# Loading the first tiles of x and w1 in another order and on other queues

## The chip, the core and the metric

The kernel runs on one core of one Trainium2 chip. The metric is the device time of one execution in microseconds (us). The engines that matter here are TensorE (PE, with weight loads on a lane of their own, PEld), VectorE (DVE), ScalarE (ACT) and the sync engine (SP), which issues transfers. Every load is done by 16 DMA engines; SP and ScalarE each have an issuing queue (q1 and q10 in the profile).

## What is computed

A gate mixes a linear-attention block with a token-mixing MLP over the same x (2048 tokens, 512 features, bf16):

```
g = sigmoid((x * gate_w).sum(-1, keepdims=True))
a = linear_attention(x, wqkv) @ wo         # 32 heads of 16, phi = elu + 1
h = layernorm(x)                           # over the 512 features
u = gelu(einsum("bsd,sf->bdf", h, w1) + b1)    # w1 is 2048 x 1792
y = einsum("bdf,fs->bds", u, w2) + b2
return g * a + (1 - g) * transpose(y)
```

The part around the change is the layer norm and the first product, h with w1, summed over the 2048 tokens.

## The kernel before

The 2048 tokens are cut into 16 tiles of 128 (`NT`). `xr` holds x, `xh` the normalised x, both 128 x 512 per tile. The columns of w1 are cut in two: `w1A` holds the first 1024 (`FA`), `w1B` the other 768, which come much later. A tile of x is 128 KB, a tile of `w1A` 256 KB. A product needs one tile of x and the same tile of w1.

**Loads.** All are recorded by the helper `load` (line 124), on SP unless another engine is named. An issue on SP takes about 0.43 us. ScalarE's queue holds, in order: a one-element square root (line 135) that brings in the activation table; the rows of b1 (136); the first 128 columns of w1's tiles 0 and 1 (137, 138). SP's queue holds x0, x1, the other 896 columns of w1's tile 0 (142), and then the loop of lines 143 to 151: x2, the rest of w1's tile 1, x3, w1's tile 2, x4, w1's tile 3, and so on, with the rows of b2 behind w1's tile 4. So every x tile from 2 on is one w1 tile ahead of its own partner. Then come the gate's row, wk, a transposed x, `w1B` and other weights.

**Order.** The order on each engine is written by hand: `tc.keep_in_program_order` (`pin`) holds every instruction where it stands. SP issues in order too, and an issue can wait for an older transfer to land.

**Layer norm.** DVE takes the tiles in turn (lines 195 to 236). `ln_bn` makes the statistics (line 198), `ln_aggr` gathers them (201) and ScalarE takes the square root (203), `ln_apply` makes the reciprocal (209) and writes `xh` (211). For tiles 1 to 3 the statistics come in two halves, and the work on the tile before is put between them. The order on DVE is therefore

```
bn(1, first half), apply(0), bn(1, second half), aggr(1),
bn(2, first half), apply(1), bn(2, second half), aggr(2),
bn(3, first half), apply(2), ...
```

At tile 8 four transposes (line 233) turn the bias rows into columns.

**Matmuls.** TensorE first runs 18 matmuls on a constant (line 189) that nothing reads. Then, for tiles 0 to 11, eight matmuls per tile (lines 276 to 278) add up into eight PSUM banks `accA`, one for each 128 columns of `w1A`; tiles 12 to 15 follow bank by bank (279 to 282), each bank ending in a gelu. All matmuls are recorded on line 74. After that come k and its products with x (`kacc`, `Gps`), the other w1 columns (`accB`), q (`qacc`), and the last stage with w2 (`yps`).

Of the kernel before, what the change touches and what calls it, by code (L numbers as in the profile page):

```python
# [7 lines left out]
ACT = mybir.ActivationFunctionType  # L8
ALU = mybir.AluOpType
AX = mybir.AxisListType  # L10
BF16 = mybir.dt.bfloat16
# [4 lines left out]
def kernel(  # L16
# [13 lines left out]
    nc = tc.nc  # L30
    P = nc.NUM_PARTITIONS
# [9 lines left out]
    NT = S // P  # L41
    ND = D // P
    NF = F // P
# [4 lines left out]
    FA = NFA * P  # L48
# [5 lines left out]
    w1_view = B_w1.rearrange("(t p) f -> p t f", p=P)  # L54
    w2_view = B_w2.rearrange("(f p) s -> p f s", p=P)
    b1_view = B_b1.rearrange("(f p) -> f p", p=P)
# [9 lines left out]
    def ptile(shape, dt, name):  # L66
        return persist.tile(shape, dt, name=name, tag=name)
# [27 lines left out]
    b_rows = ptile([32, P], BF16, "b_rows")  # L95
# [15 lines left out]
    eps_t = ptile([P, 1], FP32, "eps_t")  # L111
# [6 lines left out]
    w1A = wpool.tile([P, NT, FA], BF16, name="w1A", tag="w1st")  # L118
    w1B = wpool.tile([P, NT, F - FA], BF16, name="w1B", tag="w2nd")

    pin = tc.keep_in_program_order

    def load(o, i, eng=None, **kw):
        pin((eng or nc.sync).dma_start(out=o, in_=i, **kw))

    def load_x(t0, t1):
        load(xr[:, t0:t1, :], x_view[:, t0:t1, :])

    def load_w1a(t):
        load(w1A[:, t, :], w1_view[:, t, 0:FA])  # L130


    tbl = work.tile([P, 1], FP32, name="tbl", tag="tbl", bufs=2)
    unit = nc.const_aps.tensor(1.0, [P, 1], BF16)
    pin(nc.scalar.activation(out=tbl[:], in_=unit, func=ACT.Sqrt))
    load(b_rows[0:NF, :], b1_view, nc.scalar)
    load(w1A[:, 0, 0:P], w1_view[:, 0, 0:P], nc.scalar)
    load(w1A[:, 1, 0:P], w1_view[:, 1, 0:P], nc.scalar)

    load_x(0, 1)  # L140
    load_x(1, 2)
    load(w1A[:, 0, P:FA], w1_view[:, 0, P:FA])
    for t in range(1, NT):
        if t + 1 < NT:
            load_x(t + 1, t + 2)
        if t == 1:
            load(w1A[:, 1, P:FA], w1_view[:, 1, P:FA])
        else:
            load_w1a(t)
        if t == 4:  # L150
            load(b_rows[NF : NF + NT, :], b2_view)
    load(gw_b[:], gw_row_view.to_broadcast([P, D]))
    load(wk_sb[:], wqkv_view[:, :, D : 2 * D])
# [12 lines left out]
    for j in range(ND):  # L166
# [9 lines left out]
        out=mask[:], in_=mask[:], compare_op=ALU.is_gt, fill=1.0,  # L176
# [3 lines left out]
        out=mask[:], in_=mask[:], compare_op=ALU.is_ge, fill=0.0,  # L180
# [58 lines left out]
    tbl = work.tile([P, 1], FP32, name="tbl", tag="tbl", bufs=2)  # L239
# [98 lines left out]
    for i in range(ND):  # L338
# [4 lines left out]
            out=z_parts[:, 1, :], in0=zacc[:], in1=z_parts[:, 0, :], op=ALU.subtract  # L343
# [222 lines left out]
    t = NT - 1  # L566
# [35 lines left out]
```

## Time and profile before

| what | us |
|---|---|
| median of 3 runs | 162.99 (162.88 to 163.32) |
| the profiled execution | 163.58 |
| its span, first to last instruction | 161.8 |
| TensorE busy | 158.0 |
| VectorE busy | 118.7 |
| ScalarE busy | 53.1 |
| first matmul of `accA` | 4.91 |
| last matmul of `accA` ends | 33.51 |

Times in the views are from the start of the span. The span is 1.8 us shorter than the execution's own time, since it leaves out what lies before the first and after the last instruction. The timeline lists instructions by start and length; in brackets stands idle time ahead of one and what ended it. The chain of waits goes back from the last instruction to whatever released it. The table of stages gives the busy time of each engine in a stretch, the granted clock, the share of time that the DMA engines were busy, and GB/s. A transfer has two times: its issue on a queue, and its landing.

### The profile page before, as it was taken

The numbers are of one execution on the slowest core, as the hardware profiler recorded it, in microseconds if no ns is written. First come the engines' busy times: TensorE is split into PE (matmuls) and PEld (weight loads), VectorE is DVE, ScalarE is ACT, GpSimd is POOL, SyncE is SP. The second block draws the span as 40 slices with busy tenths as digits, with TensorE's granted clock in tenths as the row PEclk, the third lists the DMA queues.
The fourth block names the chain that finished last, engine by engine and source line by source line (L and its number), as shares of the span: only waits on it lengthen the run. The fifth ranks groups of instructions, "written<-read, shape, count | busy, mean of one in ns | idle before, by whom it ended". The sixth has DMA issues, their size and how long they took to land.

```text
span 161.8 us, 2443 instructions
## 1 busy us (share of the span) xinstructions
PE 158.0 (98%) x904; PEld 73.8 (46%) x904; DVE 118.7 (73%) x279; ACT 53.1 (33%) x89; POOL 1.2 (1%) x8
## 2 busy tenths in 40 slices
PE   7999999999999999999999999999999999999992
PEld 5344444444444444644444444444444444444452
DVE  2898998949999998799895999999999980000002
ACT  3122226895233212425234970000008300550040
POOL 2000000000000000000000000000000000000000
PEclk9999999999999999999999999999999999999999
DMA  4999999444599740225993017925349725835221
GB/s 132 277 299 347 321 322 187 100 97 97 109 391 392 214 132 0 85 54 149 377 381 65 3 36 227 324 65 162 81 86 304 276 66 140 268 95 137 80 97 32
DMA packets 36951, 28.35 MB, mean 175 GB/s; under 512 B 20556, under 2 KB 31436, under 8 KB 36940
## 3 DMA queue, kind: packets, MB, share of 16 engines
q1 hardware_dynamic: 36352, 27.87, 57.4%
q10 hardware_dynamic: 588, 0.33, 0.7%
q8 instruction: 7, 0.11, 0.3%
q14 instruction: 4, 0.03, 0.1%
HBM read 19.28 MB, written 4.46 MB: 147 GB/s over the span
## 4 chain that ended last, share of the span: by engine, by line
PE 95%; DMA 1%; DVE 1%; ACT 0%; issue 0%; DVEq 0%
PE yps L74 38%; PE accA L74 18%; PE accB L74 13%; PE qacc L74 9%; PE Gps L74 9%; PE kacc L74 9%; DMA xr<-in_A_x_dram 1%; DVE stats L198 0%; PE kvps L74 0%; DVE xh L211 0%; DVE ot L546 0%; PE w2ps L74 0%; ACT sd L203 0%; DVE mv L201 0%; DVE rstd L209 0%
## 5 line engine op out<-in xcount | busy, mean ns | idle before, releaser
L74 PE MATMUL yps<-uT,w2h 128*128 128x512 bf16 (+2 forms) x238 | 49.2, 366 | 0.0
L74 PEld LDWEIGHTS <-w2h 128*128 128x128 bf16 x238 | 22.8, 98 | 25.9
L74 PE MATMUL accA<-xh,w1A 128*128 128x512 bf16 x128 | 28.6, 387 | 0.1
L539 ACT ACTIVATE ot<-yps,c,c 128x512 bf16<-128x512 f32 x15 | 11.6, 777 | 46.9 <-PE yps L74 35.5
L74 PE MATMUL accB<-xh,w1B 128*128 128x512 bf16 (+1 forms) x144 | 21.6, 379 | 0.0
L74 PEld LDWEIGHTS <-w1A 128*128 128x128 bf16 x128 | 12.7, 99 | 16.0 <-issue 1.1
L546 DVE TENSOR_SCALAR ot<-yps,c,c 128x384 bf16<-128x384 f32 (+1 forms) x2 | 1.1, 545 | 25.5 <-PE yps L74 25.5
L74 PEld LDWEIGHTS <-xT 128*128 128x128 bf16 (+1 forms) x164 | 12.6, 97 | 14.6 <-issue 0.2
L74 PE MATMUL Gps<-pk,xr 128*128 128x512 bf16 x64 | 15.8, 379 | 0.0
L74 PE MATMUL kacc<-wk_sb,xT 128*128 128x512 bf16 x64 | 15.8, 379 | 0.0
L74 PEld LDWEIGHTS <-w1B 128*128 128x128 bf16 (+1 forms) x144 | 9.8, 98 | 10.9
L74 PE MATMUL yps<-W2sb,pqT 128*128 128x512 bf16 (+2 forms) x68 | 14.6, 366 | 0.0
L74 PE MATMUL qacc<-wq_sb,xT 128*128 128x512 bf16 (+1 forms) x100 | 14.5, 379 | 0.0
L287 ACT ACTIVATE e<-qacc 128x512 bf16<-128x512 f32 x16 | 9.6, 597 | 12.1 <-PE qacc L74 7.8
L287 ACT ACTIVATE e<-kacc 128x512 bf16<-128x512 f32 x16 | 9.2, 598 | 12.7 <-DVE pk L294 6.8
L198 DVE BATCH_NORM_STATS2 stats<-xr 128x6 f32<-128x512 bf16 (+1 forms) x19 | 11.2, 587 | 2.6 <-DMA xr<-in_A_x_dram 2.6
L289 DVE TENSOR_SCALAR e<-e 128x512 bf16<-128x512 bf16 x32 | 9.2, 288 | 4.9 <-ACT e L287 4.5
L415 DVE SCALAR_TENSOR_TENSOR pq<-pq,odds,rd 128x512 bf16<-128x512 bf16 x16 | 12.0, 752 | 0.6
L411 DVE TENSOR_REDUCE den<-prod 128x32 f32<-128x544 f32 x16 | 11.5, 720 | 0.6
L294 DVE SCALAR_TENSOR_TENSOR pk<-kacc,e 128x512 bf16<-128x512 f32 x16 | 11.1, 692 | 1.0
L294 DVE SCALAR_TENSOR_TENSOR pq<-qacc,e 128x512 bf16<-128x512 f32 x16 | 11.1, 692 | 0.8
L246 DVE CUSTOM_DVE_ANT_0 junk<-xr,gw_b 128x512 bf16<-128x512 bf16 x16 | 11.0, 690 | 0.5
(52 smaller groups left out, 95.4 us busy)
## 6 DMA issues: line engine op xcount, KB each, us to landing
w2h<-in_B_w_dram SPq DMA_DIRECT2D x4, 1792.0 KB, 8.7
w1A<-in_B_w_dram SPq DMA_DIRECT2D x14, 256.0 KB, 4.4
w1B<-in_B_w_dram SPq DMA_DIRECT2D x4, 768.0 KB, 7.4
xr<-in_A_x_dram SPq DMA_DIRECT2D x16, 128.0 KB, 4.1
q_dram<-pq SPq DMA_DIRECT2D x16, 128.0 KB, 2.0
out_dram<-ot SPq DMA_DIRECT2D x15, 128.0 KB, 1.8
wk_sb<-in_A_wqkv_dram SPq DMA_DIRECT2D x1, 512.0 KB, 6.3
wv_sb<-in_A_wqkv_dram SPq DMA_DIRECT2D x1, 512.0 KB, 11.3
```

The costliest lines, as they stand in the source:

```text
L74: nc.tensor.matmul(o, lhsT=lhsT, rhs=rhs, start=start, stop=stop, **kw)
L198: pin(nc.vector.bn_stats(out=stats[t][:, h, :], in_=xr[:, t, d0:d1]))
L246: nc.vector.tensor_tensor_reduce(out=junk[:], in0=xr[:, t, :], in1=gw_b[:], scale=1.0, scalar=0.0, op0=ALU.mult, op1=ALU.add, accum_out=gp ...
L287: pin(nc.scalar.activation(out=e[:], in_=acc[:], func=ACT.Exp))
L289: nc.vector.tensor_scalar(out=e[:], in0=e[:], scalar1=1.0, scalar2=PHI_EPS, op0=ALU.min, op1=ALU.add)
L294: nc.vector.scalar_tensor_tensor(out=o, in0=acc[:], scalar=0.0, in1=e[:], op0=ALU.max, op1=ALU.add)
L411: pin(nc.vector.tensor_reduce(out=den[:], in_=prod[:], op=ALU.add, axis=AX.X))
L415: nc.vector.scalar_tensor_tensor(out=heads, in0=heads, scalar=odds[:, t : t + 1], in1=rd[:].unsqueeze(2).to_broadcast([P, NH, HEAD]), op0= ...
L539: nc.scalar.activation(out=ot[:, d0:d1], in_=yps[:, d0:d1], func=ACT.Identity, scale=c1[:, t : t + 1], bias=c2[:, t : t + 1],)
L546: nc.vector.tensor_scalar(out=ot[:, d0:d1], in0=yps[:, d0:d1], scalar1=c1[:, t : t + 1], scalar2=c2[:, t : t + 1], op0=ALU.mult, op1=ALU.add,)
```

## The change

ScalarE's queue: the square root reads `eps_t`, which DVE writes at the start (line 115), in place of a constant; the rows of b1 leave this queue; it loads w1's tile 0 in two parts, 128 columns and then the other 896; tile 1's first columns leave it. SP's queue: x0, and then for every tile x and the whole of w1's tile, x1, w1 tile 1, x2, w1 tile 2, and so on. So x2 stands behind w1's tile 1, and every x tile right ahead of its own partner. The rows of b1 go to SP, behind w1's tile 4 and ahead of b2's.

```diff
     tbl = work.tile([P, 1], FP32, name="tbl", tag="tbl", bufs=2)
-    unit = nc.const_aps.tensor(1.0, [P, 1], BF16)
-    pin(nc.scalar.activation(out=tbl[:], in_=unit, func=ACT.Sqrt))
-    load(b_rows[0:NF, :], b1_view, nc.scalar)
+    pin(nc.scalar.activation(out=tbl[:], in_=eps_t[:], func=ACT.Sqrt))
     load(w1A[:, 0, 0:P], w1_view[:, 0, 0:P], nc.scalar)
-    load(w1A[:, 1, 0:P], w1_view[:, 1, 0:P], nc.scalar)
+    load(w1A[:, 0, P:FA], w1_view[:, 0, P:FA], nc.scalar)
 
     load_x(0, 1)
-    load_x(1, 2)
-    load(w1A[:, 0, P:FA], w1_view[:, 0, P:FA])
     for t in range(1, NT):
-        if t + 1 < NT:
-            load_x(t + 1, t + 2)
-        if t == 1:
-            load(w1A[:, 1, P:FA], w1_view[:, 1, P:FA])
-        else:
-            load_w1a(t)
+        load_x(t, t + 1)
+        load_w1a(t)
         if t == 4:
+            load(b_rows[0:NF, :], b1_view)
             load(b_rows[NF : NF + NT, :], b2_view)
```

## The prediction

> **What bounds the kernel now.** I read the page's summary of engines first: TensorE (PE) is busy 158.0 of the 161.8 us span. The chain of waits then says when the end is decided.
>
> ```profile
> 0.80 2.15 DMA xr<-in_A_x_dram
> ...
> 4.44 0.42 DVE xh L211
> 4.87 0.04 issue
> 4.91 28.60 PE accA L74 x128
> 33.51 4.32 PE kacc L74 x20
> ```
>
> Columns: start, length, what. Up to 4.87 the chain is x tile 0's load and its layer norm; from 4.91 on it is matmuls without a break. So any time that PE loses after 4.91 comes out at the end one for one, and nothing else counts. Everything the change touches happens in the first 15 us, where PE eats one tile of x and w1 per eight matmuls. The timeline of PE gives the first matmul of tiles 0 to 4 at 4.91, 7.45, 9.18, 10.90 and 12.63. Its pitch is 0.43 us until 6.57 and 0.22 after, although the stage table shows a granted clock of 1.00 in both stretches.
>
> What each tile waits for is VectorE's (DVE's) work, in program order:
>
> ```profile
> 5.23 0.21 DVE L201 BATCH_NORM_AGGREGATE mv<-stats 128x2 f32<-128x12 f32 x1
> 5.36 0.42 DVE L198 BATCH_NORM_STATS2 stats<-xr 128x6 f32<-128x256 bf16 x1
> 5.80 0.16 DVE L209 RECIPROCAL rstd<-sd 128x1 f32<-128x1 f32 x1
> 6.00 0.41 DVE L211 TENSOR_SCALAR xh<-xr,mv,rstd 128x512 bf16<-128x512 bf16 x1
> ...
> 7.30 0.43 DVE L198 BATCH_NORM_STATS2 stats<-xr 128x6 f32<-128x256 bf16 x1 [0.31 <-DMA xr<-in_A_x_dram]
> ```
>
> The instruction at 5.36 is the statistics of the first half of x tile **2**. The two behind it finish tile **1**. So x2's landing, not only x1's, gates xh tile 1. xh1 is ready at 6.41, 1.05 us after that instruction starts; PE needs it 0.06 us (4.85 to 4.91 for tile 0) before 7.45. The same sums give xh2 at 8.24 for 9.18, xh3 at 9.89 for 10.90, xh4 at 11.06 for 12.63. The slack is 0.98, 0.88, 0.95 and 1.5 us. At 7.30 x3 is already late by 0.31.
>
> Third, the queue of the sync engine (SP), and what each transfer takes to land (asked one by one):
>
> ```profile
> 1.72 0.42 SPq L124 DMA_DIRECT2D w1A<-in_B_w_dram  x1
> 2.19 0.43 SPq L124 DMA_DIRECT2D xr<-in_A_x_dram  x1
> 2.66 0.43 SPq L124 DMA_DIRECT2D w1A<-in_B_w_dram  x1
> 3.13 0.44 SPq L124 DMA_DIRECT2D xr<-in_A_x_dram  x1
> 3.62 0.43 SPq L124 DMA_DIRECT2D w1A<-in_B_w_dram  x1
> 4.87 0.33 SPq L124 DMA_DIRECT2D xr<-in_A_x_dram  x1
> ```
>
> Issue plus landing: x0 0.80+2.1=2.9, x1 1.26+2.2=3.5, w0's rest 1.72+3.1=4.8, x2 2.19+3.1=5.3, w1's rest 2.66+4.3=7.0, x3 3.13+4.1=7.2, w2 3.62+4.3=7.9, x4 4.87+3.4=8.3, x5 5.72+3.8=9.5, w4 6.20+3.9=10.1. Issues are 0.47 us apart but landings are not: the transfers queue for the 16 DMA engines. The stage table says how fast (last two columns: DMA share, GB/s).
>
> ```profile
> 4.25:4.75 0.50, 0.50 (x3) 0.21 (x2) 0.46 (x2) 0.00 (x0) 0.00 (x0) 1.00 1.13 259
> 5.25:5.75 0.50, 0.50 (x3) 0.18 (x2) 0.50 (x2) 0.28 (x1) 0.00 (x0) 1.00 0.61 157
> 6.25:6.75 0.50, 0.50 (x3) 0.16 (x2) 0.50 (x2) 0.00 (x0) 0.00 (x0) 1.00 1.09 379
> ```
>
> **The change, part by part.**
>
> *x2 behind w1 tile 1, and tile 0 on ScalarE's queue.* I count KB ahead of and including each transfer over both queues. Before, with the 67.5 KB of ScalarE's three loads: w0's rest 547 KB, landed 4.8; x2 675 KB, landed 5.3; w1's rest 899 KB, landed 7.0; x3 1027, 7.2; w2 1283, 7.9; x4 1411, 8.3; x5 1795, 9.5; w4 2051, 10.1. After: x2 has x0, x1, w1 tile 1 (256) and itself on SP, 640 KB, and w0's 256 KB on the other queue, issued earlier: 896 KB. Each later x tile has 384 KB more: x3 1280, x4 1664, x5 2048. Read off the list: x2 lands at 7.0 instead of 5.3, x3 at 7.9, x4 at 9.1, x5 at 10.1.
>
> x2's landing is the one disputed figure. From below: 221 KB more than before at the stretch's best rate (379 GB/s) is 0.6 us, so 5.9. From above: its issue stays at 2.19 and the longest landing of any x tile in this profile is 5.4, so 7.6. I take 7.0, since w1's rest holds the same byte position (899 KB) and is the nearest row; the slow 157 GB/s stretch lies in it.
>
> Then DVE: x2's first half starts at 6.99, not 5.36; xh1 is ready 1.05 later, at 8.04; PE starts tile 1 at 8.10 instead of 7.45: **0.65 us lost**. With the bounds: nothing up to a landing of 6.3, and 8.7 - 7.45 = 1.3 at 7.6. What is late next: x3's first half starts 1.55 after x2's begins without a DMA wait (x2's second half 0.97 and its aggregate 1.42 behind, then 0.13), at 8.54, later than its landing 7.9; xh2 is ready 0.94 on, at 9.48, for a PE that now comes at 9.83. x4's statistics start 1.44 after x3's, at 9.98 (landed 9.1), xh3 at 11.13 for 11.55. From there DVE takes 1.18 per tile and PE 1.73, so the lag shrinks. No second stall.
>
> *w0 in two parts on ScalarE's queue.* Its two issues cost about what the two of before cost (0.38 and 0.44). The first part, issued around 1.0 in place of 1.69, lands before 4.5, which buys nothing, since xh0 is ready only at 4.85. The rest was on SP at 1.72 and landed at 4.8; now it is issued near 1.5 and takes turns with x1 and w1 tile 1, so between 512 and 768 KB: 4.6 to 6.0. Its first matmul (the second of tile 0) starts at 5.29. A landing of 6.0 leaves seven matmuls, two at 0.43 or a little less and the rest at 0.22, and tile 1 could start near 7.88, before xh1 lets it at 8.10. So this is hidden by x2's wait; without that cover it would cost up to 0.43.
>
> [...]
>
> *x0 and the start.* x0 is issued at 0.80 as before, with 32 KB of w0 perhaps moving beside it instead of 3.5 KB: at 253 GB/s (the stretch 3.18 to 6.59) 0.1 us at most, at a point where PE runs at half pitch: under 0.1, and covered by x2's wait too.
>
> *Bias rows behind w1 tile 4.* One more SP issue of 0.33 to 0.64 ahead of x5, the durations of the two bias loads now. SP also holds back: x4 waited from 4.05 to 4.87, until w0's rest landed (the view of SP's waits has 0.8 us there, for a transfer of w1A). If x5 has to wait for x2 likewise, it is issued at 7.0, lands 3.8 later at 10.8, and is wanted at 11.13. Covered by 0.3; with the longest landing (5.4) x5 comes at 12.4 and costs 0.3 at tile 4. The bias rows are transposed at 15.04; no cost.
>
> *The activation's input.* eps_t is written at 0.99; the table load runs from 0.80 to 2.08 and the square root is first used at 3.92. Nothing, even with 0.2 us of delay.
>
> **Sum.** 0.65 us. The profiled execution took 163.58 (161.8 span and 1.8 around it), which would become 164.23; it lies 0.59 above the median 162.99 of the runs. On the median: **163.64**.
>
> **Rivals.**
>
> *Not slower (0.27, 162.99).* Place: x2's landing. If the 157 GB/s stretch is an accident of that execution, x2 lands near 5.9; from 6.3 down the slack of 0.98 swallows it all. For it: 379 GB/s a moment later. Against it: w1's rest and x3 took 4.3 and 4.1 us to land in just that byte position.
>
> *ScalarE's loads held behind its activation (0.12, 164.0).* If the queue's loads wait until the activation, now with a wait of its own, has started (2.09), w0's rest is issued near 2.7, lands in the 899 KB position, 7.0, and seven matmuls at 0.22 put tile 1 at 8.5: +1.05. Against: the bias load was issued at 1.02, long before that activation ran.
>
> *PE's fast pitch comes later (0.08, 164.7).* The gaps at tile 0 or 1 put off the change seen at 6.57. [...]
>
> *Faster (0.06).* Nothing in the change makes xh0 earlier. At most the four matmuls at 0.43 before 6.57 could come at 0.22: 0.8 less.
>
> **How the numbers follow.** The forecast has 0.47. Faster or slower by 0.3% is 0.49 us, about what a measurement here tells from no change; the forecast crosses it when x2 lands after 6.8, to which I give 0.42 of its 0.47. Slower: 0.42 + 0.12 + 0.08 = 0.62. Same: 0.05 + 0.26 = 0.31. Faster: 0.06 and 0.01 of the first rival. The range runs from the not-slower case less 0.2 (162.8) to the late pitch (164.8).
>
> **What would show it.** In the profile after: x2's first-half statistics with a DMA wait of about 1.6 us, starting near 7.0; PE idle before tile 1's first matmul near 8.1; SP's order x1, w1, x2; PE unbroken from tile 2 on. Wrong would be: a gap inside tile 0 (the second rival), x2 landed by 6.3 (the first), a pitch of 0.43 after 6.6 (the third), or a wait at x5.

## The result, and the profile after

The changed kernel takes 163.77 us (median of 22 executions, 163.10 to 166.13), the kernel before 162.91 (22, 162.67 to 163.52). The ratio is 1.0046, 95% interval 1.0033 to 1.0060: **0.75 us slower** (0.54 to 0.98). The ratio leaves out four executions from 165.76 us up, more than 1.5% above the fastest; they come up again under theory C. The profiled execution took 163.78 us, span 162.1.

The direction and the size are about those of the forecast (0.65). The place is not. In the chain of waits of the changed kernel (start, length, what), x is gone from the front:

```profile
1.47 4.51 DMA w1A<-in_B_w_dram
5.98 0.05 issue
6.03 6.65 PE accA L74 x30
```

The rest of w1's tile 0, issued on ScalarE's queue at 1.47, lands at 5.98, and the *second* matmul of tile 0 waits for it. The weight loads of TensorE (lane PEld) say the same:

```profile
4.39 0.10 PEld L74 LDWEIGHTS <-w1A 128*128 128x128 bf16 x1
6.02 7.88 PEld L74 LDWEIGHTS <-w1A 128*128 128x128 bf16 x38 [1.53 <-DMA w1A<-in_B_w_dram]
```

The reader is to see one load, 1.53 us of nothing, and then an unbroken row. The first matmul ran at 4.91 as before, so matmuls stood still from 5.3 at the latest to 6.03. VectorE's timeline shows the wait that the forecast had named:

```profile
5.22 0.21 DVE L194 BATCH_NORM_AGGREGATE mv<-stats 128x2 f32<-128x12 f32 x1
6.32 0.43 DVE L191 BATCH_NORM_STATS2 stats<-xr 128x6 f32<-128x256 bf16 x1 [0.89 <-DMA xr<-in_A_x_dram]
6.67 0.15 DVE L202 RECIPROCAL rstd<-sd 128x1 f32<-128x1 f32 x1
6.85 0.41 DVE L204 TENSOR_SCALAR xh<-xr,mv,rstd 128x512 bf16<-128x512 bf16 x1
```

x2's first statistics start at 6.32 instead of 5.36, and xh of tile 1 is ready at 7.26, 0.94 later. But PE comes to tile 1 only at 7.55, so in this execution that wait costs nothing.

The stage table (last columns: clock, DMA share, GB/s) shows what went with x2's coming sooner than the forecast's 7.0. The slow half microsecond has moved:

```profile
3.25:3.75 0.50, 0.50 (x4) 0.33 (x3) 0.47 (x2) 0.00 (x0) 0.00 (x0) 1.00 0.57 77
5.25:5.75 0.50, 0.04 (x1) 0.00 (x0) 0.18 (x1) 0.28 (x1) 0.00 (x0) 1.00 1.08 401
6.25:6.75 0.50, 0.50 (x4) 0.26 (x3) 0.43 (x2) 0.00 (x0) 0.00 (x0) 1.00 1.08 404
```

It stands at 3.25 with 77 GB/s, where before it stood at 5.25 with 157. This goes with the order of the loads more than with the execution. In e10 below, which begins with the loads of the kernel before, it stands at 5.25 again, and in e6 and e7, with the same loads, the slowest stretch behind 3.25 is at 4.75 (191 and 183). In all six profiles that have the rest of tile 0 on ScalarE's queue (the changed kernel, e1, e3, e5, e9, e11) it stands at 3.25, with 63 to 167 GB/s, and at 5.25 the engines move 320 to 401. From e10 and e11:

```profile
5.25:5.75 0.50, 0.50 (x3) 0.25 (x2) 0.49 (x2) 0.27 (x1) 0.00 (x0) 1.00 0.53 161
```

```profile
3.25:3.75 0.50, 0.50 (x4) 0.34 (x3) 0.47 (x2) 0.00 (x0) 0.00 (x0) 1.00 0.60 73
```

**Two executions are not alike.** Tile 1 starts at 7.55 here and started at 7.45 in the profile before: 0.10 later, where the medians differ by 0.75. The two profiles differ in PE's pitch. Before, it was 0.43 us until 6.57. Here it is 0.22 already at 6.03 (the starts are 6.03, 6.25, 6.47, 6.68). With a pitch of 0.216 from its first matmul on, the kernel before would have come to tile 1 at 4.91 + 8 x 0.216 = 6.64, 0.81 earlier than it did; and 0.85 is how far its 22 executions lie apart. So I compare like with like, first by an estimate. With the early pitch the loss is 7.55 - 6.64 = 0.91. With the late one the changed kernel's matmuls would start at 6.03, 6.46, 6.73 and then every 0.216, tile 1 at 7.81: 0.36. The mean, 0.64, lies in the measured interval.

Two later profiles make the comparison without a sum. e10 begins with the loads of the kernel before, e11 with those of the changed kernel, and in both the pitch is 0.22 from the third matmul on. The weight loads of e10 and then e11, from the second matmul on:

```profile
5.30 0.15 PEld L74 LDWEIGHTS <-w1A 128*128 128x128 bf16 x1 [0.28 <-issue]
5.64 6.36 PEld L74 LDWEIGHTS <-w1A 128*128 128x128 bf16 x30 [0.18 <-issue]
```

```profile
6.08 5.94 PEld L74 LDWEIGHTS <-w1A 128*128 128x128 bf16 x29 [1.51 <-DMA w1A<-in_B_w_dram]
```

Tile 1 starts at 6.93 in e10 and at 7.61 in e11, 0.68 later, and the two executions took 162.97 and 163.71 us, 0.74 apart.

### The profile page after: what moved, and what is told of

The parts are those of the page before. It is cut to its first block, busy times and chain, and to the rows that moved or that the text cites. A ratio compares the mean times of both kernels' runs of the same rounds, so it can differ in the third digit from the quotient of the medians.

```text
span 162.1 us, 2429 instructions
## 1 busy us (share of the span) xinstructions
PE 156.6 (97%) x891; PEld 73.4 (45%) x904; DVE 118.7 (73%) x279; ACT 53.1 (33%) x89; POOL 1.2 (1%) x8
## 4 chain that ended last, share of the span: by engine, by line
PE 94%; DMA 3%; issue 1%; ACT 0%; DVE 0%; DVEq 0%
PE yps L74 38%; PE accA L74 17%; PE accB L74 13%; PE kacc L74 9%; PE qacc L74 9%; PE Gps L74 8%; DMA w1A<-in_B_w_dram 3%; ACT L134 0%; PE kvps L74 0%; DVE ot L539 0%; PE w2ps L74 0%; DVEq L539 0%
## 5 line engine op out<-in xcount | busy, mean ns | idle before, releaser
L74 PE MATMUL accA<-xh,w1A 128*128 128x512 bf16 x126 | 27.9, 379 | 1.1 <-DMA w1A<-in_B_w_dram 0.7
```

The lines of the kernel that those rows point to most:

```text
L74: nc.tensor.matmul(o, lhsT=lhsT, rhs=rhs, start=start, stop=stop, **kw)
```

## The experiments

Three theories. **X**: x2's landing holds tile 1, by VectorE's program order. **W**: the rest of w1's tile 0 lands too late on ScalarE's queue. **C**: gaps on PE put off the fast pitch. Each ratio is to the kernel before, run on the same chip.

### e1: x one ahead again, w0 stays on ScalarE's queue

```diff
     load_x(0, 1)
+    load_x(1, 2)
     for t in range(1, NT):
-        load_x(t, t + 1)
+        if t + 1 < NT:
+            load_x(t + 1, t + 2)
         load_w1a(t)
```

> The changed kernel with one part undone: on SP every x tile from 2 on is again one w1 tile ahead (x0, x1, x2, w1 tile 1, x3, ...); w1's tile 0 stays in two parts on ScalarE's queue. Theory X (x2's landing gates tile 1): x2 lands by 5.7, no gap before tile 1, time within 0.2 us of the kernel before. Theory W (the rest of w1's tile 0, sharing the DMA engines with SP's transfers, gates the second matmul): it still lands between 5.4 and 6.0, PE still idles inside tile 0 for 0.2 to 0.7 us, and 0.3 us or more of the 0.8 us loss stays. Theory C (PE's gaps put off the fast pitch in some executions): executions over 164.5 us stay as long as the gap inside tile 0 stays.

Measured: 163.54 us, ratio 1.0026 (1.0009 to 1.0042), 0.42 us slower. PE's weight loads:

```profile
4.42 0.15 PEld L74 LDWEIGHTS <-w1A 128*128 128x128 bf16 x1
5.71 6.37 PEld L74 LDWEIGHTS <-w1A 128*128 128x128 bf16 x31 [1.14 <-DMA w1A<-in_B_w_dram]
```

With x back in front, the second matmul still waits, until 5.71 (issue 1.47, landing 4.2). X alone would have brought the time back; it didn't. By the same sum as above, tile 1 comes at 5.71 + 7 x 0.216 = 7.22 for 6.64 with the early pitch, 0.58, and at 7.67 for 7.45 with the late one, 0.22. W explains what stayed. No execution of 12 was over 164.1, where C had expected long ones as long as the gap inside tile 0 stays.

### e2: w0's rest back on SP, x2 stays behind w1's tile 1

```diff
     load(w1A[:, 0, 0:P], w1_view[:, 0, 0:P], nc.scalar)
-    load(w1A[:, 0, P:FA], w1_view[:, 0, P:FA], nc.scalar)
     load_x(0, 1)
+    load_x(1, 2)
+    load(w1A[:, 0, P:FA], w1_view[:, 0, P:FA])
     for t in range(1, NT):
-        load_x(t, t + 1)
+        if t > 1:
+            load_x(t, t + 1)
         load_w1a(t)
```

> The changed kernel with the other part undone: the rest of w1's tile 0 goes back to SP, behind x1; x2 stays behind w1's tile 1. Theory X: x2 lands between 6.3 and 7.0, PE idles before tile 1, 0.3 to 0.9 us slower than the kernel before. Theory W: the rest of tile 0 lands near 4.8, there is no gap inside tile 0, and the time is within 0.2 us of the kernel before. Theory C: a gap of under 0.8 us between tiles 0 and 1 leaves few or no executions over 164.5 us.

Measured: 163.48 us, ratio 1.0023 (1.0009 to 1.0038), 0.37 us slower. The two views that matter, VectorE's and PE's:

```profile
6.25 0.43 DVE L193 BATCH_NORM_STATS2 stats<-xr 128x6 f32<-128x256 bf16 x1 [0.76 <-DMA xr<-in_A_x_dram]
6.78 0.41 DVE L206 TENSOR_SCALAR xh<-xr,mv,rstd 128x512 bf16<-128x512 bf16 x1
```

```profile
5.18 0.32 PEld L74 LDWEIGHTS <-w1A 128*128 128x128 bf16 x2 [0.61 <-DMA w1A<-in_B_w_dram]
5.77 0.15 PEld L74 LDWEIGHTS <-w1A 128*128 128x128 bf16 x1 [0.28 <-issue]
```

On SP, issued at 1.72, 0.25 later than on ScalarE's queue, the rest of tile 0 lands at 5.1, where it landed at 5.7 in e1 and at 6.0 in the changed kernel, and tile 0 has no gap. x2 lands at 6.25, and xh1 is ready at 7.19. This execution had the late pitch (until 6.53); PE came to tile 1 at 7.39 and lost nothing. With the early one it would have waited from 6.64 to 7.25, 0.61 by the estimate above. A mean of 0 and 0.61 lies within the measured 0.15 to 0.62. So both parts cost by themselves, about 0.4 us each: neither X alone nor W alone holds. (Both kernels hold the small parts of e4 as well.)

### e3: 23 matmuls on the constant in place of 18

```diff
-    for _ in range(18):
+    for _ in range(23):
```

> The changed kernel with 23 instead of 18 matmuls on the constant at the start, so that TensorE is busy until about 5.9 us instead of 4.8 and the first matmul of tile 0 comes right behind. Theory C: the executions over 164.5 us go, the lower ones stay near 163.7. Theories X and W alone: the loads are as late as before, the first matmul slips by at most the time it had to wait anyway, and the spread of executions (163.1 to 166.1) stays.

Measured (on the changed kernel): 163.75 us, ratio 1.0043 (1.0028 to 1.0059); 12 executions from 163.37 to 164.32. PE was busy until 5.7, the first matmul of tile 0 came there and the second at 6.13. The median is that of the changed kernel, as X and W say, and there is no long execution, as C says; the spread up to 166.1 that X and W alone expected did not come. But e5 below has none in ten with 18, so twelve without one settle nothing.

### e4: the small parts alone

The kernel before with `eps_t` as the activation's input and b1's rows behind w1's tile 4 on SP.

```diff
-    pin(nc.scalar.activation(out=tbl[:], in_=unit, func=ACT.Sqrt))
-    load(b_rows[0:NF, :], b1_view, nc.scalar)
+    pin(nc.scalar.activation(out=tbl[:], in_=eps_t[:], func=ACT.Sqrt))
...
         if t == 4:
+            load(b_rows[0:NF, :], b1_view)
             load(b_rows[NF : NF + NT, :], b2_view)
```

> The kernel before with only the two small parts of the change: the activation at the start reads eps_t, and the rows of b1 go to SP behind w1's tile 4. All theories: within 0.2 us of the kernel before. [...]

Measured: 163.30 us, ratio 1.0008 (0.9988 to 1.0027), 0.13 us slower (-0.20 to 0.44). No difference that this shows. In the changed kernel's profile x5's statistics start at 10.47 without a wait, as forecast.

### e5: the changed kernel again

> The changed kernel as it is, once more, beside the two below. Theory C (a gap on PE puts off the fast pitch in some executions): again one execution in four or so is 1.5 to 2.5 us above the others. Rival: those long executions came from the first measurement's surroundings; none here above 164.6.

Measured: 163.75 us, ratio 1.0046 (1.0028 to 1.0064), ten executions from 163.24 to 164.36. The loss is the same; the long executions didn't come. They did come in e9 (one of 12, 165.74) and e11 (two of 12, 165.42 and 165.53), and never in the 24 executions of e2 and e8, with w0's rest on SP, nor in e1 or e4. The profile shows a third way for the same loads to be late:

```profile
4.55 0.43 DVE L191 BATCH_NORM_STATS2 stats<-xr 128x6 f32<-128x256 bf16 x1 [0.77 <-DMA xr<-in_A_x_dram]
5.07 0.41 DVE L204 TENSOR_SCALAR xh<-xr,mv,rstd 128x512 bf16<-128x512 bf16 x1
```

Here it is **x1** that came late (issue 1.27, landing 3.3, where it was 2.2 before). Its first half stands ahead of tile 0's reciprocal on VectorE, so xh0 came at 5.48 instead of 4.85 and the first matmul at 5.54.

### e6 and e7: a gap on PE alone

The kernel before, loads untouched, with fewer matmuls on the constant, so that PE idles before 4.9.

```diff
-    for _ in range(18):
+    for _ in range(13):   # e7: 15
```

> The kernel before with 13 instead of 18 matmuls on the constant: its loads are untouched, but TensorE idles from about 3.7 to 4.9 us. Theory C: the median or at least some executions go up by 0.8 to 2 us, and matmuls keep the 0.43 us pitch past 6.6 us in the profile of such an execution. Rival (late loads alone make the long executions, a gap costs only its own length): time within 0.2 us of the kernel before, since the first real matmul still starts at 4.91.

> The same with 15: a gap of about 0.75 us, near the 0.7 us that the changed kernel has inside tile 0. Theory C: some executions 1.5 to 2 us above the others, fewer than with 13. Rival: within 0.2 us of the kernel before, no long executions.

e6 measured 164.79 us, ratio 1.0106 (1.0088 to 1.0125), 1.7 us slower: removing work that nobody reads makes the kernel slower. e7's 11 executions (median 164.42) fall in two groups: five from 162.77 to 162.88, six from 164.42 to 165.22. PE's weight loads of the profiled executions, e6 and then e7 (lines left out are alike):

```profile
4.86 0.10 PEld L74 LDWEIGHTS <-w1A 128*128 128x128 bf16 x1 [0.47 <-DMA w1A<-in_B_w_dram]
5.24 0.15 PEld L74 LDWEIGHTS <-w1A 128*128 128x128 bf16 x1 [0.28 <-issue]
...
7.80 0.15 PEld L74 LDWEIGHTS <-w1A 128*128 128x128 bf16 x1 [0.27 <-issue]
8.23 3.79 PEld L74 LDWEIGHTS <-w1A 128*128 128x128 bf16 x18 [0.28 <-issue]
```

```profile
9.31 0.15 PEld L74 LDWEIGHTS <-w1A 128*128 128x128 bf16 x1 [0.28 <-issue]
9.74 2.29 PEld L74 LDWEIGHTS <-w1A 128*128 128x128 bf16 x11 [0.27 <-issue]
```

Single loads 0.43 apart are the slow pitch; the merged row (18 loads in 3.79 us, 0.21 each) is the fast one. It begins at 8.23 and 9.74, in place of 6.57 or earlier. The first matmul was on time in e6 (4.86). So the gap of e6 (1.09 us in the profile) costs nothing by its length and 1.7 us by the pitch, and that of e7 (0.75 us by the estimate, 0.88 in the profiled execution, where the first columns of w1 landed at 5.0) does it in six of 11 executions. C's mechanism is shown. That it makes the changed kernel's long executions is argued only: 1.5 to 2 us is the right size and the gap inside tile 0 is 0.7 us or more in the profiles of the changed kernel and e11, but no such execution was profiled.

What decides when the fast pitch sets in, no run here shows. It came at 6.57 in the profile of the kernel before and at 5.64 in e10's, with the same start, and e7's executions, of one kernel, fall at 162.8 and at 164.4 to 165.2 us.

### e8 and e9: VectorE's order alone

In the kernel of e2 (e8) and in the changed kernel (e9), tile 1's reciprocal and xh go ahead of tile 2's statistics. The loads stay.

```diff
+        if t == 2:
+            ln_apply(1)
+            ln_bn(2, 0, D // 2, 0, 2)
+            ln_bn(2, D // 2, D, 1, 2)
-        if t < HALVES:
+        elif t < HALVES:
```

> The kernel of e2 (rest of w1's tile 0 on SP, x2 behind w1's tile 1), with one change on VectorE alone: tile 1's reciprocal and xh come ahead of tile 2's first statistics instead of behind. The loads are those of e2. Theory X, as far as it says that program order on VectorE lets x2 hold tile 1: xh of tile 1 is ready near 6.5 whenever x2 lands, PE starts tile 1 without a wait, and most of e2's 0.37 us loss goes (within 0.2 us of the kernel before; tile 2's xh comes some 0.2 us later than in the kernel before and may cost that in executions with an early fast pitch). Rival (e2's loss comes from something else, the DMA stage as a whole): 0.3 to 0.5 us slower than the kernel before, as e2.

> The changed kernel with the same reordering on VectorE. Theory W (the rest of w1's tile 0 lands last): the loss of 0.75 us stays for the most part, 0.5 to 0.8 us slower than the kernel before, with the gap inside tile 0. Theory X alone: it falls to 0.2 us or less.

e8 measured 163.12 us, ratio 1.0010 (0.9997 to 1.0022): of e2's 0.37 us, 0.16 (-0.05 to 0.36) is left. VectorE's timeline of e8:

```profile
6.06 0.41 DVE L206 TENSOR_SCALAR xh<-xr,mv,rstd 128x512 bf16<-128x512 bf16 x1
6.39 0.74 DVE L193 BATCH_NORM_STATS2 stats<-xr 128x6 f32<-128x256 bf16 x2
```

xh1 is ready at 6.47 while x2's statistics come behind. PE's weight loads run on without a break from 5.23 to 8.37. Tile 2 then starts at 8.62 in place of 8.49, since xh2 is ready at 8.57; these 0.13 are about what is left. So the rows show X's cost as the program order on VectorE, not the DMA stage as a whole; by the times alone the intervals of e2 (0.15 to 0.62) and e8 overlap.

e9 measured 163.70 us, ratio 1.0038 (1.0024 to 1.0052): 0.62 (0.39 to 0.85) of the 0.75 stays. X contributes little to the changed kernel, because PE is held longer by W (in e5 by x1 first): in its four profiles with the old order on VectorE (the changed kernel, e3, e5, e11) xh1 is ready at 7.26, 7.33, 7.06 and 7.42, and PE starts tile 1 only at 7.55, 7.65, 7.26 and 7.61. e1 leaves 0.42 (0.15 to 0.68) for W, so its share is known no better than 0.4 to 0.6. The profiled execution of e9 was a lucky one (163.00): there the rest of tile 0 landed at 5.1, issue 1.48 and landing 3.6, where other profiles have 4.1 to 4.6.

### e10 and e11: a second wait, at 129 us

The forecast said that PE would be unbroken from tile 2 on. That does not hold in every execution. The wait lists between 128 and 130 us, of the changed kernel and of e1 (waiting, released by, us in total, times, longest):

```profile
PEld L74 <- DMA w2h<-in_B_w_dram: 0.4, 1, 0.4
```

```profile
PEld L74 <- DMA w2h<-in_B_w_dram: 0.9, 1, 0.9
PE yps L74 <- DMA w2h<-in_B_w_dram: 0.4, 1, 0.4
```

The last quarter of w2 is issued behind VectorE's last stage at 118.8 to 121.1 and lands 8.3 to 10.2 us later; PE wants it 9.3 to 9.5 after its issue. From the end of `accA` to the last matmul eleven of the thirteen profiles take 125.4 to 125.5 us, the changed kernel's among them; e1's takes 0.57 us more than the one before and e5's 0.38. In the others at most the weight loads wait, and PE loses next to nothing. In e10 (on the kernel before) and e11 (on the changed one) it is loaded in two transfers:

```diff
-    pieces = {0: ((0, 7),), 7: ((7, NF),)}
+    pieces = {0: ((0, 7),), 7: ((7, 9), (9, NF))}
```

> The kernel before with the last quarter of w2 (row blocks 7 to 13 of its second half) loaded in two transfers, blocks 7 and 8 and then the rest, in place of one that takes 8.3 to 10.2 us to land while PE wants it 9.3 to 9.5 us after its issue. If PE's wait of 0.4 to 0.9 us for w2 at 129 us, seen in four profiles, is paid in part of the executions of every kernel: 0.1 to 0.3 us faster than the kernel before, and no wait for w2 in the profile. Rival (the wait comes with the change alone): no difference.

> The changed kernel with the same cut of w2's last quarter. If the wait for w2 is a matter of every kernel, this is 0.1 to 0.3 us faster than the changed kernel's 163.75, and its distance to e10 stays near 0.75 us. Rival (part of the 0.75 us is that wait): its distance to the kernel before falls to 0.5 or less while e10 gains nothing.

e10 measured 162.79 us, ratio 0.9984 (0.9965 to 1.0002); the profile still has a weight load that waits 0.2 us for w2. e11 measured 163.70, ratio 1.0048 (1.0017 to 1.0079). A gain of the size expected in e10, but the interval includes none; in e11 nothing that can be seen. The distance of the changed kernel from the one before stays, 0.78 us in e11. So the wait is not seen to be part of the 0.75 us. That the kernel before pays it in some executions, as e10 supposed, is not shown: of the five profiles with its order (before, e4, e6, e7, e10) none loses time to it. Whether the cut is worth having is open.

## Why the prediction came out, step by step

**PE bounds, and a loss in the first tiles ends up in the time: right.** What e11's profile loses against e10's, 0.68 us at tile 1, arises in the first 8 us and is there at the end (0.74 in the time), since the stretch behind `accA` takes the same time in both. "Matmuls without a break" passed over the wait at 129 us in e1 and e5.

**x2's landing at 7.0: too late.** Its statistics could start at 6.3 in the changed kernel, e2 and e3 (6.32, 6.25, 6.39), at 6.48 in e11 and by 6.12 in e5. The figure was read off the byte position of w1's rest. That landing is no accident of one execution (6.6 to 7.1 in before, e6, e7 and e10), but it belongs to the old order of loads: with tile 0 on ScalarE's queue the same bytes come sooner, and the slow stretch lies at 3.25 and not at 5.25. So the first rival's reason, an accident of that execution, does not hold either, though x2 landed near its 6.3. 5.9 to 7.6 was the stated range.

**x2 gates xh1 through VectorE's order: right in kind** (e2 and e8), but it was priced against a PE at the late pitch. With the early one PE wants tile 1 at 6.64 by the estimate (6.80 in e4's profile, 6.93 in e10's) and not at 7.45, so 6.3 costs 0.3 to 0.6, not nothing. The early pitch comes in the kernel before too, so it is no gain of the change, as the forecast's "faster" case had it.

**w0's rest hidden by x2's wait: the step that failed.** The forecast had 4.6 to 6.0, and 0.43 without cover. It landed at 5.98, the end of that range, and it covers x2's wait, not the other way round. e1, with x2's order restored, still loses 0.42 us. On SP, behind x0 and x1, tile 0's rest had SP's later transfers behind it: in the kernel before it landed at 4.86 and x2, issued 0.47 later, at 5.32. On the other queue it shares the DMA engines with them: in the changed kernel it landed at 5.98, and the 256 KB of w1's tile 1, issued on SP 0.25 later, at 6.13. From 3.75 to 4.25 SP's queue took 45.2% of the 16 engines and ScalarE's 31.2%, from 4.25 to 4.75 57.3% and 33.5%. The forecast counted the KB of both queues in one line as an estimate; that the two queues' packets move in the same half microseconds, the profile before shows too (81.0% and 24.2% from 3.75 to 4.25). Issued at 1.47 on ScalarE's queue, it lands at 5.1 to 6.1 (the changed kernel, e1, e3, e5, e9, e11); issued at 1.72 on SP, at 4.5 to 5.2 (the kernel before, e2, e4, e6, e7, e8, e10). ScalarE's queue is not slow as such: in the changed kernel its first 32 KB, issued at 1.04, landed in 2.13 us, x0, issued on SP at 0.80, in 2.15.

**x0 and the start: right for x0 (landing 2.2 for 2.1), incomplete for the start.** x1, which also stands ahead of xh0, can be late (e5).

**Bias rows and the activation's input: no cost, right** (e4). The load on ScalarE's queue went out at 1.04, a microsecond ahead of the activation:

```profile
1.04 0.89 ACTq L124 DMA_DIRECT2D w1A<-in_B_w_dram  x2
2.08 0.20 ACT L134 ACTIVATE tbl<-eps_t 128x1 f32<-128x1 f32 x1
```

That closes the rival in which the loads are held behind it. The sign that the forecast gave for it, a gap inside tile 0, did appear, from the sharing of the engines.

**The late pitch, given 0.08,** is a real mechanism (e6, e7), and likely the long executions, 8 of the 56 of the changed kernel, e5, e9 and e11 at 165.3 or more. It isn't in the median. The size that the forecast gave it, 164.7, rests on a delay of the fast pitch that no run shows; the fast pitch came at 8.23 in e6's profile and at 9.74 in e7's, for 6.57, and e6's median is 1.7 us above the kernel before. So 0.65 was near 0.75 partly by luck: a wait overpriced by 0.7 us of landing, another dismissed, and both weighed against one execution's pitch.

## What to carry to other kernels

Here the first thing needed, moved to a second queue, was issued at 1.47 instead of 1.72 and landed at 5.98 instead of 4.86: it lost its place in the line, and the transfers it used to be ahead of shared the DMA engines with it (57.3% and 33.5% from 4.25 to 4.75). A step priced as hidden by a wait has to be priced without it too, and a single profile asked what in it is a draw of that execution and what belongs to the order of the kernel: here PE's pitch in the first tile differed from execution to execution (0.43 or 0.22 us) and decided how much a wait cost (0.36 or 0.91 us by the estimate), while the slow half microsecond of DMA came back with each order of loads (at 5.25 before and in e10 and at 4.75 in e6 and e7 with the old one, at 3.25 with tile 0's rest on ScalarE's queue), so that the landings of the old order were no measure for the new one.

## What the runs showed of the hardware that was not expected

- In e7 a gap on PE ahead of the first matmul of `accA`, 0.88 us in the profile, made 6 of 11 executions 1.6 to 2.4 us longer than the others; in e6 one of 1.09 us made all six measured at least 1.4 us longer than the kernel before's median.
- The stage table's clock column reads 1.00 in the kernel before while matmuls of 512 columns start every 0.43 us up to 6.57, and 1.00 when they start every 0.22; the pitch of the weight loads is the better witness.
- The DMA engines together fall to a low rate for half a microsecond in the first 6 us, at a place that goes with the order of the loads: 157 and 161 GB/s at 5.25 (before, e10), 63 to 167 at 3.25 in the six profiles with tile 0's rest on ScalarE's queue, which then move 320 to 404 from 4.75 to 6.75. What makes the dip is not shown.
